# Agent attention with two MLPs on one core: a timetable's list drives the first sixteen steps and the weight conversions, without the clamp and without the pool engine

## The chip, the cores and the metric

The kernel runs on one core of a Trainium2 chip. The metric is the device time of one execution in microseconds, and every time here is of that kind. Five engines appear: TensorE (PE in the profile; PEld is its weight load), VectorE (DVE), ScalarE (ACT), GpSimd (POOL) and SyncE (SP), whose queue issues almost all DMAs.

## What is computed

The reference is an attention through 49 agents, and after it two feed-forward layers on all 12480 tokens of 128 channels:

```python
a2k = sm(agents, k)                 # 49 agents look at 12480 keys
agent_v = a2k @ v                   # 49 x 128
q2a = sm(q, agents)                 # each token looks at the 49 agents
x = q2a @ agent_v
x = maximum(x @ w_in, 0)**2 @ w_out             # first layer, 2048 hidden
h = x @ w_in2                                   # second layer, 2048 hidden
y = (maximum(h, 0) + alpha * minimum(h, 0)) @ w_out2
```

Here `sm` is a softmax over scaled products. The four weight matrices lie in DRAM as 64-bit floats, and the kernel makes 32-bit floats of them on the chip; everything else is float32.

## The kernel before

**The fold.** The product `agent_v @ w_in` is made once (49 x 2048, called W1), so that the first layer's hidden values of a token are its softmax row times W1. The leaky relu of the second layer is split into `(1-alpha) * relu(h)` and a linear part: w_out2 is scaled by 1-alpha (`oma`), and M = w_in2 · diag(alpha) · w_out2 (128 x 128) is made once and applied to x directly.

**Precision.** Operands of the large products are split into a high and a low part in the fp32r format (a cast, then a subtraction), and three products hi·lo, lo·hi, hi·hi are added up. So each operand costs a cast (ACT, or DVE for `g1h`) and a subtraction.

**The weights.** Each of the four matrices comes in four parts of 128x512 numbers, named `wi1.0` to `wo2.3` (in the trace all parts pass through the buffers raw, mag and wf). A part goes through these steps, each a letter ahead of its name in the order lists:
- d (`w_load`, L131 to L149): a 512 KB DMA into one of six `raw` slots, two int32 halves to a number;
- a (`w_abs`, L152, ACT): absolute value of the upper half, read as a float, into one of two `mag` slots;
- m (`w_max`, L156, POOL): a clamp from below at 2^-15, so that the exponent can be shifted in place;
- b (`w_bits`, L160, L161, L164, DVE): shift and mask, put the sign in, put the low half's bits in, to one of five `wf` slots; the `raw` and `mag` slots are free after it;
- s (`w_scale`, L392, POOL), for wo2 only: times 1-alpha, into another `wf` slot;
- h (`w_hi`, L399, ACT) and l (`w_lo`, L403, POOL): the high part and the low part, for wo1, wi2 and wo2 (W1 has its own, L649 on ACT and L652 on DVE);
- t, y (`m_transpose`, L415, PE; `m_alpha`, L421, DVE), for wi2: transposed, times alpha, into mT; z, w (`m_product`, PE; `m_add`, L439 and on, DVE): M's partial product and its sum.

**Attention.** Keys and values come in 13 chunks each (`ring<-in_k_dram`, `ring<-in_v_dram`, 512 KB apiece). A chunk of keys is transposed (T, C), multiplied with the agents (S), gets a running maximum and an exponential (X, P and the line L549, L553, L560), is turned (E, F: L570, L577) and multiplied with its chunk of values (M). At the end the 49 x 128 result is normalised (N, L620), transposed (vT) and copied as `avT` (vc, L635), from which W1 is made (W0, W1, with Y and Z for its two parts).

**The steps.** The tokens are cut into 25 blocks (320 tokens, then 512 each, 384 in the last), and each block takes 8 steps, 200 in all. A step s does H1 (first layer, products of W1 and the softmax rows `qsh`, `qsl` into `h_ps`), relu (L756, ACT), square (L876, ACT), G1 (cast L764 and subtraction L765, DVE), and, two steps later, O (the second product). Eleven steps behind H1 comes H2 of the second layer (relu L819 on ACT, L820 on DVE), and one step behind that its O. All matmuls go through `mm` (L78).

**What sets the order.** Scheduling is by hand: each engine executes its instructions in the order in which the program issues them. Before the loop a written list, ORDER, interleaves the attention, the first query blocks (names beginning with q) and the conversion of wi1 and wo1 and of a part of wi2. The rest of the conversions, of wi2 and wo2, stands in a table LATER, by the steps 0 to 13 behind which they are issued. Loads stand in the list too, so SP's queue follows it: its DMAs are issued in order, and one that waits for its slot holds those behind it.

**PSUM.** ORDER runs in a pool `early`; the loop's pool opens when ORDER is done, and with it the SBUF pools `wk` and `xp` of the loop.

Of the kernel before, what the change touches and what calls it, by code (L numbers as in the profile page):

```python
# [19 lines left out]
def agent_attention_moe_kernel(  # L20
# [96 lines left out]
    HI_KEEP = -(1 << 30)  # L117
    MIN_HI = 2.0 ** -15
# [4 lines left out]
    wf = Slots(stg, 5, [QW], F32, "wf")  # L123
# [46 lines left out]
    with tc.manual_schedule(), ExitStack() as first:  # L170
        early = first.enter_context(tc.tile_pool(name="early", bufs=1, space=PSUM))
# [218 lines left out]
        def w_scale(x):  # L390
            g = int(x[4:])
            nc.gpsimd.tensor_tensor(  # L392
# [14 lines left out]
        wT, mP = {}, {}  # L407
# [25 lines left out]
        def m_add(x):  # L433
            g = int(x[4:])
            p_ = mP.pop(g)
            if g == 0:
# [50 lines left out]
        kT_ps, kT_sb, s_ps, ex_sb, e_ps, e_sb, q_ps, out_ps = {}, {}, {}, {}, {}, {}, {}, {}  # L487
# [86 lines left out]
        def e_copy(c):  # L574
            p, t = shape(c)
            e_sb[c] = att.tile([128, KC // 2, 2, H], F32, tag="e1", name="e1", bufs=3)[:p, :t]
            nc.scalar.copy(e_sb[c].rearrange("p j r a -> p (j r a)"), e_ps.pop(c))  # L577

        def av_chunk(c):
            p, t = shape(c)  # L580
            g = GROUP[c]
            e, v_ = e_sb.pop(c), chunk("v", c)
# [101 lines left out]
        def q_end(b):  # L684
# [8 lines left out]
            "T": q_turn, "h": q_first_hi, "l": q_first_lo, "s": q_scores, "t": q_squares, "m": q_max, "u": q_sub,  # L693
# [240 lines left out]
```

## Time and profile before

| | us |
|---|---|
| runs | 1127.34, 1125.65, 1119.55 |
| median | 1125.65 |
| profiled execution | 1119.32 |
| its span in the trace | 1117.5 |
| around the span | 1.8 |
| mean granted PE clock | 0.982 |

The span is cut by the profile's page into 40 slices of 28 us. PE, at work nearly all the time, is not so only in the first six slices; the work that the change touches lies there. Where a busy time and a number of instructions stand together, the number is behind an x. "Granted clock" is the share of full speed (2.4 GHz) that PE was given; 0.5 is the lower of its two levels.

### The profile page before, as it was taken

The page shows a single profiled execution, that of the slowest core. Times are in us where ns is not written, and L with a number is a line of the kernel's source. Part 1 is how long each engine was busy: PE and PEld are TensorE (multiplying, and loading weights), DVE is VectorE, ACT ScalarE, POOL GpSimd, SP SyncE. Part 2 cuts the span into 40 slices and gives each one's busy share as a digit, 9 for nine tenths or more (in the row PEclk, how much of TensorE's full clock was granted, in tenths as well). Part 3 has the DMA queues.
Part 4 walks back from the last instruction along what each step waited for, and adds up shares of the span by engine and source line. Part 5 has one row for each costly group of instructions (what it writes and reads, how often), then busy time and mean ns, then how long its engine had stood idle before and what let it go on. Part 6 is the DMA issues. An engine that isn't in the chain of part 4 may idle for free.

```text
span 1117.5 us, 22093 instructions
## 1 busy us (share of the span) xinstructions
PE 1072.9 (96%) x9368; PEld 859.8 (77%) x9368; DVE 897.9 (80%) x1377; ACT 728.9 (65%) x835; POOL 46.8 (4%) x38
## 2 busy tenths in 40 slices
PE   8868699999999999999999999999999999999997
PEld 5546588888888888888888888888888888888886
DVE  6778787887887888887888788788788888788753
ACT  5656376666666666666667667666766676766642
POOL 1353300000000000000000000000000000000000
PEclk9978799999999999999999999999999999999999
DMA  9941011111111111111111111111111111001011
GB/s 348 322 126 23 1 30 17 29 34 22 27 35 29 20 29 30 20 29 29 20 30 29 20 29 32 17 31 37 20 26 33 29 18 29 20 11 29 20 24 18
DMA packets 119931, 48.19 MB, mean 43 GB/s; under 512 B 103640, under 2 KB 109337, under 8 KB 119833
## 3 DMA queue, kind: packets, MB, share of 16 engines
q1 hardware_dynamic: 119832, 46.79, 17.6%
q8 instruction: 73, 1.20, 0.5%
q14 instruction: 26, 0.20, 0.1%
HBM read 27.59 MB, written 6.39 MB: 30 GB/s over the span
## 4 chain that ended last, share of the span: by engine, by line
PE 88%; DVE 7%; ACT 2%; issue 1%; DMA 1%; SPq 0%; POOL 0%; DVEq 0%; ACTq 0%
PE o L78 49%; PE h_ps L78 36%; PE s_ps L78 2%; DVE g1l L765 1%; DVE mag L161 1%; PE M_ps L78 1%; DVE wf L164 1%; DVE g1h L764 1%; DVE mag L160 1%; DVE mx L549 0%; DVE g2l L820 0%; PE warm_ps L78 0%; SPq L244 0%; ACT kT L533 0%; ACT g L876 0%
## 5 line engine op out<-in xcount | busy, mean ns | idle before, releaser
L756 ACT ACTIVATE g<-h_ps 128x1024 f32<-128x1024 f32 (+2 forms) x200 | 201.0, 1005 | 177.3 <-PE h_ps L78 176.5
L819 ACT ACTIVATE g2h<-h_ps 128x1024 fp32r<-128x1024 f32 (+2 forms) x200 | 201.5, 1007 | 151.4 <-PE h_ps L78 132.7
L820 DVE SCALAR_TENSOR_TENSOR g2l<-h_ps,g2h 128x1024 fp32r<-128x1024 f32 (+2 forms) x200 | 238.2, 1191 | 21.0 <-ACT g2h L819 21.0
L765 DVE TENSOR_TENSOR g1l<-g,g1h 128x1024 fp32r<-128x1024 f32 (+2 forms) x200 | 242.6, 1213 | 6.9
L764 DVE CAST g1h<-g 128x1024 fp32r<-128x1024 f32 (+2 forms) x200 | 136.8, 684 | 111.5 <-ACT g L876 110.6
L876 ACT ACTIVATE g<-g 128x1024 f32<-128x1024 f32 (+2 forms) x200 | 207.8, 1039 | 6.4
L78 PE MATMUL o<-g1h,wo1l 64*128 64x512 f32 (+2 forms) x800 | 158.1, 392 | 0.0
L78 PE MATMUL o<-g2l,wo2h 64*128 64x512 f32 (+2 forms) x800 | 157.5, 389 | 0.5 <-DVE g2l L820 0.5
L78 PE MATMUL o<-g2h,wo2h 64*128 64x512 f32 (+2 forms) x800 | 157.5, 389 | 0.0
L78 PE MATMUL o<-g1h,wo1h 64*128 64x512 f32 (+2 forms) x800 | 157.4, 390 | 0.0
L78 PE MATMUL o<-g1l,wo1h 64*128 64x512 f32 (+2 forms) x800 | 157.1, 389 | 0.1
L78 PE MATMUL o<-g2h,wo2l 64*128 64x512 f32 (+2 forms) x800 | 156.4, 386 | 0.0
L78 PEld LDWEIGHTS o<-g1l,wo1h 64*128 64x128 f32 x800 | 76.4, 188 | 17.9 <-DVE g1l L765 0.3
L78 PEld LDWEIGHTS o<-g1h,wo1h 64*128 64x128 f32 x800 | 76.5, 188 | 17.3
L78 PEld LDWEIGHTS o<-g2h,wo2l 64*128 64x128 f32 x800 | 76.3, 186 | 17.3 <-ACT g2h L819 0.2
L78 PEld LDWEIGHTS o<-g2l,wo2h 64*128 64x128 f32 x800 | 75.9, 185 | 17.3 <-DVE g2l L820 0.8
L78 PEld LDWEIGHTS o<-g1h,wo1l 64*128 64x128 f32 x800 | 76.3, 187 | 16.8
L78 PEld LDWEIGHTS o<-g2h,wo2h 64*128 64x128 f32 x800 | 75.9, 185 | 16.4
L78 PE MATMUL h_ps<-qsh,W1l 64*128 64x512 f32 (+2 forms) x400 | 80.8, 401 | 7.3 <-DVE W1l L652 2.8
L78 PE MATMUL h_ps<-xh,wi2l 64*128 64x512 f32 (+2 forms) x400 | 79.3, 392 | 1.2 <-DVE g2l L820 1.2
L78 PE MATMUL h_ps<-sl,wi2h 64*128 64x512 f32 (+2 forms) x400 | 79.4, 390 | 0.4 <-DMA sl<-xl 0.4
L78 PE MATMUL h_ps<-sh,wi2l 64*128 64x512 f32 (+2 forms) x400 | 79.2, 389 | 0.4 <-DMA sh<-xh 0.4
(142 smaller groups left out, 1476.1 us busy)
## 6 DMA issues: line engine op xcount, KB each, us to landing
ring<-in_k_dram SPq DMA_DIRECT2D x12, 512.0 KB, 7.9
ring<-in_v_dram SPq DMA_DIRECT2D x12, 512.0 KB, 6.8
sh<-xh SPq DMA_DIRECT2D x46, 128.0 KB, 2.4
sl<-xl SPq DMA_DIRECT2D x46, 128.0 KB, 2.3
out_dram<-ot SPq DMA_DIRECT2D x92, 64.0 KB, 2.0
q_sb<-in_q_dram SPq DMA_DIRECT2D x176, 32.0 KB, 1.9
raw<-in_moe_w_in_dram SPq DMA_DIRECT2D x4, 512.0 KB, 10.0
raw<-in_moe_w_out_dram SPq DMA_DIRECT2D x4, 512.0 KB, 9.2
```

The source lines that it names most:

```text
L78: nc.tensor.matmul(o, lhsT, rhs, start=start, stop=stop)
L160: nc.vector.tensor_scalar(a, a, 3, 0x3FFFFFF8, op0=ALU.logical_shift_left, op1=ALU.bitwise_and)
L161: nc.vector.scalar_tensor_tensor(out=a, in0=hi, scalar=HI_KEEP, in1=a, op0=ALU.bitwise_and, op1=ALU.bitwise_or)
L164: nc.vector.scalar_tensor_tensor(out=dst.bitcast(I32), in0=lo, scalar=29, in1=a, op0=ALU.logical_shift_right, op1=ALU.bitwise_or)
L756: nc.scalar.activation(g, p_, AF.Relu)
L764: nc.vector.tensor_copy(gh, g)
L765: nc.vector.tensor_tensor(out=gl, in0=g, in1=f32(gh), op=ALU.subtract)
L819: nc.scalar.activation(gh, p_, AF.Relu)
L820: nc.vector.scalar_tensor_tensor(out=gl, in0=p_, scalar=0.0, in1=f32(gh), op0=ALU.max, op1=ALU.subtract)
L876: nc.scalar.activation(h1g[s], h1g[s], AF.Square)
```

## The change

One list now covers what ORDER and LATER held and the first sixteen steps (blocks 0 and 1) besides: H1 to H1_15, the first products O1 up to step 13, H2 up to step 4 and O2 up to step 3, and the third query block's softmax. The loop begins at step 16. For that the step functions are cut into pieces that a list can name (`H1_0`, `r1_0` relu, `s1_0` square, `c1_0` and `x1_0` G1's cast and subtraction, and so on). The order inside the list is new. The other edits:
- The absolute value is multiplied by 2^-112 (`REBIAS`), the clamp is gone, the shift has no mask, and the sign is taken with a mask of the top bit.
- `w_scale` (four instructions) and `w_lo` (twelve) are on DVE; nothing of the weights is left on POOL.
- `m_alpha`: each of its four DVE instructions of 128x512 becomes four on ACT of 128x128, with alpha as the scale of each partition.
- `wf` has six slots in place of five.
- M's partial products are added up in the order in which they come.
- The early PSUM pool closes before W1's product, which takes a bank of the loop's pool; the attention's SBUF pool closes at PART2.

```diff
-    wf = Slots(stg, 5, [QW], F32, "wf")
+    wf = Slots(stg, 6, [QW], F32, "wf")
...
     def w_abs(x):
-        nc.scalar.activation(mag.take(x).bitcast(F32), raw.get(x)[:, :, 1].bitcast(F32), AF.Abs)
-
-    def w_max(x):
-        m = mag.get(x).bitcast(F32)
-        nc.gpsimd.tensor_scalar(m, m, MIN_HI, None, op0=ALU.max)
+        nc.scalar.activation(mag.take(x).bitcast(F32), raw.get(x)[:, :, 1].bitcast(F32), AF.Abs, scale=REBIAS)
...
-        nc.vector.tensor_scalar(a, a, 3, 0x3FFFFFF8, op0=ALU.logical_shift_left, op1=ALU.bitwise_and)
+        nc.vector.tensor_scalar(a, a, 3, None, op0=ALU.logical_shift_left)
         nc.vector.scalar_tensor_tensor(
-            out=a, in0=hi, scalar=HI_KEEP, in1=a, op0=ALU.bitwise_and, op1=ALU.bitwise_or
+            out=a, in0=hi, scalar=SIGN, in1=a, op0=ALU.bitwise_and, op1=ALU.bitwise_or
         )
...
         def w_scale(x):
-            nc.gpsimd.tensor_tensor(
+            nc.vector.tensor_tensor(
...
+        LO_VECTOR = 'wo1.0 wo1.1 wo1.2 wo1.3 wi2.0 wi2.1 wi2.2 wi2.3 wo2.0 wo2.1 wo2.2 wo2.3'.split()
         def w_lo(x):
             hi, lo = halves(x)
-            nc.gpsimd.tensor_tensor(out=lo, in0=source(x), in1=f32(hi), op=ALU.subtract)
+            e = nc.vector if x in LO_VECTOR else nc.gpsimd
+            e.tensor_tensor(out=lo, in0=source(x), in1=f32(hi), op=ALU.subtract)
...
         def m_alpha(x):
-            a = alp.rearrange("p (i r) -> p r i", r=2)[:, :, 2 * g:2 * g + 2]
-            nc.vector.tensor_tensor(
-                out=mT[:, g], in0=wT.pop(g), in1=a.unsqueeze(3).to_broadcast([128, 2, 2, 128]), op=ALU.mult
-            )
+            p_ = wT.pop(g)
+            for i in range(2):
+                for r in range(2):
+                    k = 4 * g + 2 * i + r
+                    nc.scalar.activation(mT[:, g, r, i], p_[:, r, i], AF.Copy, scale=alp[:, k:k + 1])
...
         ORDER = """
...
+            R5 bwo1.3 hwo1.0 M11 dwo2.1 awo2.0 E12 hwi2.2 dwo2.2 R6 F12 N2 hwo1.3 M12 awi2.3 dwo2.3 R7 bwi2.3 vT
+            vc hwi2.3 lwo1.3 PART1 W0 awo2.3 bwo2.0 W1 Y0 Z0 awo2.1 swo2.0 PART2 H1_0 Y1 q2 lwo1.0 r1_0 Z1
...
-        LATER = {
...
+        S0 = 2 * NP
+        pend = [S0 - D - 1]
-        for s in range(S + D + 2):
+        for s in range(S0, S + D + 2):
...
-            for x in LATER.get(s, "").split():
-                step(x)
```

On DVE, around the begin of the steps (first the four H1 products of width 320: `g_888`, `g_864` and the like are the relu'd hidden values of one step each), the kernel before has this:

```order
L421 TENSOR_TENSOR mT<-wT_ps,alp 128x512
L652 TENSOR_TENSOR W1l<-w_ps,W1h 128x512 x2
L764 CAST g1h<-g_888 128x2x320
L765 TENSOR_TENSOR g1l<-g_888,g1h 128x2x320
L160 TENSOR_SCALAR mag<-mag 128x512
L161 SCALAR_TENSOR_TENSOR mag<-raw,mag 128x512
L164 SCALAR_TENSOR_TENSOR wf<-raw,mag 128x512
L764 CAST g1h<-g_915 128x2x320
L765 TENSOR_TENSOR g1l<-g_915,g1h 128x2x320
```

and the changed kernel this:

```order
L654 TENSOR_TENSOR W1l<-w_ps,W1h 128x512
L389 TENSOR_TENSOR wf<-wf,oma 128x512
L403 TENSOR_TENSOR wo1l<-wf,wo1h 128x512
L654 TENSOR_TENSOR W1l<-w_ps,W1h 128x512
L156 TENSOR_SCALAR mag<-mag 128x512
L157 SCALAR_TENSOR_TENSOR mag<-raw,mag 128x512
L160 SCALAR_TENSOR_TENSOR wf<-raw,mag 128x512
L770 CAST g1h<-g_864 128x2x320
L775 TENSOR_TENSOR g1l<-g_864,g1h 128x2x320
L770 CAST g1h<-g_897 128x2x320
L775 TENSOR_TENSOR g1l<-g_897,g1h 128x2x320
L403 TENSOR_TENSOR wi2l<-wf,wi2h 128x2x256
```

The alpha product left DVE, a scale (L389) and low parts (L403) joined it, and a conversion now stands ahead of the first step's cast where it stood behind its subtraction.

On ACT at the same place, from W1's high parts to the first steps' relu and square, before:

```order
L649 CAST W1h<-w_ps 128x512
L399 CAST wi2h<-wf 128x2x256
L649 CAST W1h<-w_ps 128x512
L152 ACTIVATE mag<-raw 128x512
L756 ACTIVATE g_888<-h_ps 128x2x320
L876 ACTIVATE g_888<-g_888 128x2x320
L756 ACTIVATE g_915<-h_ps 128x2x320
L876 ACTIVATE g_915<-g_915 128x2x320
```

and in the changed kernel:

```order
L651 CAST W1h<-w_ps 128x512
L152 ACTIVATE mag<-raw 128x512
L651 CAST W1h<-w_ps 128x512
L759 ACTIVATE g_864<-h_ps 128x2x320
L396 CAST wo2h<-wf 128x512
L763 ACTIVATE g_864<-g_864 128x2x320
L759 ACTIVATE g_897<-h_ps 128x2x320
L763 ACTIVATE g_897<-g_897 128x2x320
L424 ACTIVATE mT<-wT_ps,alp 128x128 x4
L759 ACTIVATE g_932<-h_ps 128x2x320
```

A high part (L396) now stands between the first step's relu and its square, and the four alpha products (L424) ahead of the third step's relu.

On SP, its queue from the second part of wo1 on, before:

```order
L141 DMA raw<-in_moe_w_out_dram 128x4x256
L481 DMA ring<-in_k_dram 128x1024 x2
L481 DMA ring<-in_v_dram 128x1024 x2
L141 DMA raw<-in_moe_w_out_dram 128x4x256 x2
L139 DMA raw<-in_moe_w_in_dram 64x512 x16
L149 DMA raw<-in_moe_w_out_dram 128x2x256 x8
L244 DMA q_sb<-in_q_dram 32x8x32 x24
```

and in the changed kernel from the first part of wi2 on (`64x512` is a quarter of a part of wi2, L149 half a part of wo2):

```order
L139 DMA raw<-in_moe_w_in_dram 64x512 x4
L483 DMA ring<-in_k_dram 128x1024
L141 DMA raw<-in_moe_w_out_dram 128x4x256
L483 DMA ring<-in_v_dram 128x1024 x2
L139 DMA raw<-in_moe_w_in_dram 64x512 x8
L141 DMA raw<-in_moe_w_out_dram 128x4x256
L483 DMA ring<-in_v_dram 128x1024
L149 DMA raw<-in_moe_w_out_dram 128x2x256 x2
L483 DMA ring<-in_v_dram 128x1024
L139 DMA raw<-in_moe_w_in_dram 64x512 x4
L483 DMA ring<-in_v_dram 128x1024
L149 DMA raw<-in_moe_w_out_dram 128x2x256 x6
```

The last chunks of K and V stood ahead of all loads of wi2 and wo2; now all of wi2 and a part of wo2 stand ahead of the last V chunk.

## Rows read from the trace of the kernel before

**Rows 1.** Page: busy us, share of the span and instructions by engine.
```profile
PE 1072.9 (96%) x9368; PEld 859.8 (77%) x9368; DVE 897.9 (80%) x1377; ACT 728.9 (65%) x835; POOL 46.8 (4%) x38
```

**Rows 2.** Windows: us, busy PE, PEld, DVE, ACT, POOL, PEclk, DMA share, GB/s.
```profile
7.23:148.03 140.80, 106.73 (x921) 78.50 (x921) 112.21 (x220) 82.76 (x129) 46.08 (x32) 0.87 0.47 153
146.22:1117.50 971.28, 961.93 (x8446) 779.99 (x8442) 785.82 (x1146) 645.54 (x703) 0.00 (x0) 1.00 0.14 26
...
77.00:102.00 25.00, 18.00 (x184) 15.11 (x184) 21.36 (x33) 18.65 (x26) 8.39 (x6) 0.85 0.18 28
102.00:137.90 35.90, 24.85 (x166) 20.11 (x166) 27.99 (x44) 14.49 (x19) 13.25 (x10) 0.74 0.04 10
```

**Rows 3.** Timeline of PE: start, duration, what; the bracket: idle before it, releaser.
```profile
134.32 1.16 PE L78 MATMUL M_ps<-wf,mT 128*128 128x128 f32 x8 [3.79 <-DVE g2l L820]
135.86 2.08 PE L78 MATMUL M_ps<-wf,mT 128*128 128x128 f32 x8 [0.38 <-DVE Mf L439]
137.86 0.79 PE L78 MATMUL h_ps<-qsh,W1l 64*128 64x512 f32 x2
146.22 0.40 PE L78 MATMUL h_ps<-qsh,W1l 64*128 64x512 f32 x2
```

**Rows 4.** Waits, 7.23 to 148.7: engine, line, releaser: us, times, longest.
```profile
PE M_ps L78 <- DVE g2l L820: 10.0, 2, 6.2
...
DVE g1h L764 <- ACT g L876: 6.9, 5, 2.4
DVE mx L549 <- PE s_ps L78: 6.3, 3, 2.9
...
DVE agTh L508 <- ACT agT L501: 4.3, 1, 4.3
```

**Rows 5.** Groups by form on DVE, 7.23 to 148.03: busy us, mean ns | idle before.
```profile
L161 DVE SCALAR_TENSOR_TENSOR mag<-raw,mag 128x512 int32<-128x512 int32 x16 | 12.1, 755 | 0.5
L765 DVE TENSOR_TENSOR g1l<-g,g1h 128x1024 fp32r<-128x1024 f32 x8 | 11.7, 1461 | 0.3
L765 DVE TENSOR_TENSOR g1l<-g,g1h 128x640 fp32r<-128x640 f32 x8 | 7.6, 947 | 0.3
...
L553 DVE SCALAR_TENSOR_TENSOR nm<-mx,nm 128x1 f32<-128x1 f32 x7 | 3.0, 422 | 0.2
L421 DVE TENSOR_TENSOR mT<-wT_ps,alp 128x512 f32<-128x512 f32 x4 | 2.7, 686 | 1.6 <-PE wT_ps L415 1.6
L370 DVE TENSOR_TENSOR qsl<-e,qsh 128x512 fp32r<-128x512 f32 x2 | 1.4, 680 | 0.0
```

**Rows 6.** Timeline of DVE: start, duration, what.
```profile
50.25 0.16 DVE L553 SCALAR_TENSOR_TENSOR nm<-mx,nm 128x1 f32<-128x1 f32 x1
...
50.95 0.69 DVE L161 SCALAR_TENSOR_TENSOR mag<-raw,mag 128x512 int32<-128x512 int32 x1
...
82.82 0.82 DVE L765 TENSOR_TENSOR g1l<-g,g1h 128x640 fp32r<-128x640 f32 x1
84.09 1.80 DVE L765 TENSOR_TENSOR g1l<-g,g1h 128x640 fp32r<-128x640 f32 x1
...
98.41 1.23 DVE L765 TENSOR_TENSOR g1l<-g,g1h 128x1024 fp32r<-128x1024 f32 x1
```

**Rows 7.** Timeline of POOL: start, duration, what, idle before it and releaser.
```profile
83.74 1.46 POOL L403 TENSOR_TENSOR wi2l<-wf,wi2h 128x512 fp32r<-128x512 f32 x1 [5.48 <-ACT wi2h L399]
```

**Rows 8.** Windows: the attention, ended by 69.12, and two within; columns as in rows 2.
```profile
7.23:69.12 61.89, 48.83 (x449) 32.46 (x447) 49.58 (x124) 38.68 (x69) 20.05 (x14) 0.96 0.89 310
10.00:20.00 10.00, 8.84 (x93) 5.58 (x93) 6.57 (x21) 6.40 (x13) 1.49 (x1) 1.00 1.04 397
40.00:50.00 10.00, 6.53 (x50) 3.72 (x47) 6.95 (x11) 5.50 (x9) 2.44 (x3) 1.00 1.04 328
```

**Rows 9.** Page, DMA issues: how often, KB each, us to landing.
```profile
ring<-in_v_dram SPq DMA_DIRECT2D x12, 512.0 KB, 6.8
```

**Rows 10.** Groups by form on ACT, 7.23 to 148.03: busy us, mean ns | idle.
```profile
L577 ACT COPY e<-e_ps 96x128 f32<-96x128 f32 x1 | 0.3, 261 | 1.1 <-PE e_ps L570 1.1
```

More of the change, by code (lines that the diff above doesn't have):

```diff
@@ L170, in agent_attention_moe_kernel @@
     with tc.manual_schedule(), ExitStack() as first:
-        early = first.enter_context(tc.tile_pool(name="early", bufs=1, space=PSUM))
+        early_pool = first.enter_context(ExitStack())
+        early = early_pool.enter_context(tc.tile_pool(name="early", bufs=1, space=PSUM))
         att = first.enter_context(tc.tile_pool(name="att", bufs=1))
@@ L435, in m_add @@
             p_ = mP.pop(g)
-            if g == 0:
+            if not m_done:
                 nc.vector.tensor_copy(Mf, p_[:, :C])
@@ L581, in av_chunk @@
             g = GROUP[c]
-            e, v_ = e_sb.pop(c), chunk("v", c)
+            e, v_ = e1_sb.pop(c), chunk("v", c)
             for j in range(t):
@@ L641, in w1_product @@
             if g == 0:
-                out_ps["w1"] = early.tile([128, 2, NT], F32, tag="kT", name="w1_ps")
+                out_ps["w1"] = ps("h2", "w1_ps")
             p_ = out_ps["w1"][:, g].rearrange("p (i m) -> p i m", m=128)
@@ L708, in step @@
                 weight(x)
+            elif "_" in x:
+                LOOP[x[:2]](int(x[3:]))
+            elif x[:2] in X_STEPS:
+                X_STEPS[x[:2]](int(x[2:]))
             elif x[0] == "q":
-                if x[1].isdigit():
-                    q_first(int(x[1]))
+                if not x[1].isdigit():
+                    Q_STEPS[x[1]](int(x[2:]))
+                elif int(x[1:]) < 2:
+                    q_first(int(x[1:]))
                 else:
-                    Q_STEPS[x[1]](int(x[2:]))
+                    q_load(int(x[1:]))
             elif x[0] in "KV":
@@ L791, in X1_add, with X1_part, X1_swap, X1_hi @@
             nc.vector.tensor_tensor(out=x1[b], in0=x1[b], in1=o1p.pop(b)[:, 1], op=ALU.add)
-        def X1(b):
+        def X1_part(b, tag, swapped):
+            return [pools["xp"].tile([128, NT], F32R, tag=t, name=t)[:, :width(b)] for t in (tag, swapped)]
+        def X1_swap(a, o):
+            for r in range(2):
+                nc.sync.dma_start(out=f32(o[rows(r)]), in_=f32(a[rows(1 - r)]))
+        def X1_hi(b):
             x = x1[b]
-            n = width(b)
-            xh, sh, xl, sl = (xp.tile([128, NT], F32R, tag=t, name=t)[:, :n] for t in ("xh", "sh", "xl", "sl"))
+            xh, sh = X1_part(b, "xh", "sh")
             nc.scalar.copy(xh, x)
+            X1_swap(xh, sh)
+            x1[b] = x, xh, sh
+        def X1_lo(b):
+            x, xh, sh = x1[b]
+            xl, sl = X1_part(b, "xl", "sl")
             nc.vector.tensor_tensor(out=xl, in0=x, in1=f32(xh), op=ALU.subtract)
-            for a, o in ((xh, sh), (xl, sl)):
-                for r in range(2):
-                    nc.sync.dma_start(out=f32(o[rows(r)]), in_=f32(a[rows(1 - r)]))
+            X1_swap(xl, sl)
             x1[b] = (xh, sh), (xl, sl)
@@ L842, in agent_attention_moe_kernel @@
+        """
+        for x in ORDER.split():
+            step(x)
         before = {
@@ L880, in agent_attention_moe_kernel @@
                 X1_copy(bx)
-            if i == 1 and s >= NP:
+            if i == 1:
                 q_scores(b + 1)
@@ L897, in agent_attention_moe_kernel @@
                 OUT(bo)
-            for f, ahead in after.get(i, ()) if s >= NP else after_0.get(i, ()):
+            for f, ahead in after.get(i, ()):
                 f(b + ahead)
@@ L901, in agent_attention_moe_kernel @@
                 q_load(b + 3)
-            for x in LATER.get(s, "").split():
-                step(x)
 _INS = ["q", "k", "v", "agents", "moe_w_in", "moe_w_out", "moe2_w_in", "moe2_w_out", "moe2_alpha"]
```

143 lines of the change are left out of this document (81 added, 62 removed).

## Prediction

> **What bounds the kernel now.** I read first the busy times of the engines: PE is at work for 1072.9 us, far ahead of DVE's 897.9 [rows 1]. So I looked next for where PE is not busy. The windows say it: from 146.22 us on, where H1 of step 16 starts, PE works 961.93 of 971.28 us at full clock [rows 2]. The code behind that point is the same in both kernels, since the new loop begins with that step. What the change can win or lose is the place of that one matmul in time: the time after is 1119.3 (the profiled execution's own) less 146.2, plus the time at which step 16's H1 starts, plus what that stretch loses behind it.
>
> Then I asked who sets the 146.2. From 7.23 to 148.03 DVE is busy 112.21 of 140.80 us, PE 106.73 at a mean clock of 0.87, ACT 82.76, POOL 46.08 [rows 2]. No engine is full; DVE comes nearest. The list of waits agrees: PE's longest ones for M's products are for DVE, 10.0 us in two waits, and DVE itself waits for ACT's squares (6.9) and for PE's scores (6.3) [rows 4]. I read the stretch as DVE's work plus DVE's waits, 112.2 and 28.6, in an order that lets neither cover the other.
>
> Third, DVE's own groups. Some durations are too long for their size: the subtraction L765 of 128x640 takes 0.947 on average [rows 5], but 0.82 alone at 82.82 and 1.80 at 84.09 [rows 6], when POOL was at a subtraction from 83.74 to 85.20 [rows 7]. L553, one column wide, takes 0.422 on average and 0.16 alone [rows 5, 6]. DVE loses time beside POOL.
>
> **The change part by part, on DVE.** Its work before is 112.2.
> - Added: 12 low parts and 4 scales, 128x512 each, from POOL. The nearest row is L370, the same operation, size and types: 680 ns [rows 5]; 16 x 0.68 = 10.9. From below, 0.82 for 640 columns scaled to 512 gives 0.66, so 10.5; from above, the disturbed 0.947 gives 15.2. I take 10.9.
> - Removed: four alpha products, 4 x 0.686 = 2.7 [rows 5].
> - Stretches that go with POOL's work, mean less alone [rows 5, 6]: L765 of 1024, 8 x (1.461 - 1.23) = 1.85; L765 of 640, 8 x (0.947 - 0.82) = 1.0; L553, 7 x (0.422 - 0.16) = 1.8; L161, 16 x (0.755 - 0.69) = 1.0. Together 5.7.
> - The shift has one operation instead of two. No row shows that form. Of a part's three DVE instructions the dearest row is L161's 0.755; a third off that for 16 parts would be 4.0 won, and equally much lost if the single form were dearer. I take 0, as the size and the types stay.
>
> Sum: 112.2 + 10.9 - 2.7 - 5.7 = 114.7.
>
> On the stretches the Trainium skill ("SBUF — State Buffer", section "SBUF: two separate sides") has a rule: DVE and GpSimd share a port pair as an exclusive lock, held for a whole instruction, and a DVE operation with two SBUF inputs meets it. By the rule all such stretches end with an idle POOL, and the sum would be the 114.7; if they had another cause it would be 120.4, a rival below. The 1.80 against 0.82 speaks for the rule.
>
> **DVE's waits** were 28.6. The order on record shows the means to cut them: a conversion (three instructions that need only a landed weight) stands ahead of the first step's cast, where DVE before went from conversion to cast and back only between steps. Waits of the kind that such work fills are the 6.9 and the 6.3 [rows 4]. The 4.3 for the agents' transpose [rows 4] stands at the very start, before a part of the weights has been converted, and stays. So the bounds are 4.3 below and 28.6 - 13.2 = 15.4 above; I take 6, near the lower end, as stretches of the groups that I did not list still sit inside the 114.7 and come off too. DVE starts at 7.2, so it is through at 7.2 + 114.7 + 6 = 127.9, and I let step 16's H1 start there: 18.3 earlier.
>
> **The other engines.** ACT gets 16 products of 128x128 for alpha. The nearest row is a copy of 96x128, 261 ns [rows 10]: 16 x 0.26 = 4.2, at worst 16 x 0.69 = 11. ACT is idle for 58 of 140.8 us [rows 2], which hides either; behind them in its queue stands the third step's relu, so if they come late PE's H1 bank is late by the four of them, 1.0. The scale in the absolute value is an argument of the same instruction: 0, and the clamp's instructions were POOL's, whose idleness costs nothing but ends one link of each conversion. The sixth wf slot and the order of M's sum remove waits only. The pool PART1 opens earlier makes W1's product wait for the last users of the early banks; it waited for them before as well: 0.
>
> SP's queue is where the change takes a risk: all of wi2 and a part of wo2 stand ahead of the last V chunk. By my count 20 MB must then have landed before the attention can end. In full use the DMA engines moved 397 GB/s at 10 to 20 us and 328 at 40 to 50 [rows 8]: 50 or 61 us from 7.2 on, so V's last chunk lands between 58 and 68. Before, the attention ended at 69.1, with DVE busy 49.58 of 61.89 [rows 8]; with its waits cut it would end near 62. I take the faster end, since the contiguous K and V chunks carry most bytes, and charge nothing.
>
> **PE's clock.** When PE stands still the granted clock falls and what follows is slow: M's product takes 2.08 where the one before took 1.16, and H1's first pair at 137.86 takes 0.79 against 0.40 at 146.22 [rows 3]. A list that keeps DVE full will still leave PE short of work for a while, and some of that return to full clock may fall behind the common point: four such matmul pairs, 4 x 0.39, are 1.5 lost.
>
> In all 18.3 - 1.5 = 16.8, so 1119.3 - 16.8 = 1102.5; I say 1102. The profiled execution lies at the low end of the runs, 6 below their median of 1125.65; a median that stood so to it would be 1108, within the range. About 1% (11.3 us) is what a measurement of this kernel can tell from no change, so faster means below 1114.4. With the bounds of the main case (waits 4.3 to 15.4, prices -0.4 to +4.3, the shift ±4) it goes from 1096 to 1112 and, with wholly unlisted stretches, to 1090.
>
> **Rivals.**
> *The loads come late.* For it: the mean of the whole attention was 310 GB/s, not 397 [rows 8], and 20 MB at that rate take 64.5 us, so V's end lands at 71.7 where I need some 62. Against it: the engines were in full use in both stretches, so the mean holds waits for slots. Price 71.7 - 62 = 9.7: 1112.
> *The change does not do what it says*: the stretches were not POOL's. Then 5.7 come back: 1108. Against it are the two L765 side by side [rows 6, 7].
> *PE at its lower clock becomes the bound.* PE's work from 77 to 137.9 is 18.00 x 0.85 + 24.85 x 0.74 = 33.7 at full clock [rows 2], and 8.4 follow to 146.22 [rows 3]: 42.1, or 84.2 at the lower level, 1.2 GHz. If the attention ends at 62 and PE never has work enough to be raised, step 16 starts at 62 + 84.2 = 146.2, as before: 1119. For it: in 102 to 137.9, where PE was busy 24.85 of 35.9, the clock was 0.74 [rows 2]. Against it: at 40 to 50 PE was busy 6.53 of 10 at 1.00 [rows 8], and a denser list keeps it busier than now.
> The Trainium skill ("TensorE: Matmul & The Clock Gate", section "Part 1: The HAM clock gate") puts it that "the default state is throttled, and activity releases the throttle". The 0.74 agrees; the 1.00 at a busy share below it does not by itself.
> *Slower: the SP queue blocks.* A weight's load waits for a raw slot that only a DVE conversion frees; with seven such loads ahead of K or V chunks, each wait holds a chunk, and the conversion that would free the slot is queued on DVE behind attention work that needs the chunk. One held chunk costs at most its landing, 6.8 [rows 9]: 7 x 6.8 = 47.6, less what DVE can convert meanwhile, six slots of 3 x 0.755 = 13.6, makes 34 and 1136. It decides against the change from 16.8 us of net waits on; by 28 it is slower by over 1%. Against it: six raw slots, as before, and a list that places each conversion.
>
> **How the numbers follow.** Main 0.68, late loads 0.14, stretches not POOL's 0.06, lower clock 0.08, blocked queue 0.04. Faster by over 1% are the main case, the stretches and part of the late loads: 0.80. Within 1%: the rest of the late loads and the lower clock, 0.15. Slower: 0.05. The range, 1090 to 1118, holds the first three and leaves out the clock's and the queue's, and the outer ends of the main one.
>
> **What would show it.** Step 16's H1 near 128 in place of 146.2. DVE busy for about 115 from 7 to there, with L765 of 640 at 0.82 and 1024 at 1.23, and the low parts at 0.68. DVE's waits below 15. The attention's last copy (avT) near 62; if it is at 69 or later and the last V chunk is what it waited for, the loads were the rival. A clock below 0.7 from the first step to step 16 with PE busy throughout shows the clock's. I am wrong if DVE has over 25 us of waits there, or if PE is no longer full behind step 16.

## The result, and the profile after

The changed kernel takes 1108.26 us (median of four runs, 1106.78 to 1109.29) against 1126.05 for the kernel before (the three runs above and a fourth of 1126.44): a ratio of 0.9852, 95% interval 0.9813 to 0.9892. It is faster, by 1.5%; 1102 was forecast, in a range of 1090 to 1118. The profiled execution took 1108.75 with a span of 1106.9, which is 10.6 less than the span before. That the medians lie 17.8 apart and the two traces 10.6 comes from the runs of the kernel before, and is looked at below.

The page's busy times of the changed kernel answer to [rows 1]:

```profile
PE 1072.7 (97%) x9368; PEld 857.5 (77%) x9368; DVE 893.0 (81%) x1389; ACT 732.2 (66%) x851; POOL 0.7 (0%) x6
```

PE's work is the same, and POOL is empty as the change says. The windows answer to [rows 2] (same columns). Step 16's H1 starts at 133.35 here and avT's copy at 70.60:

```profile
7.20:133.35 126.15, 102.67 (x905) 73.69 (x903) 106.14 (x230) 85.20 (x144) 0.00 (x0) 0.91 0.57 173
133.35:1106.90 973.55, 963.98 (x8442) 780.90 (x8442) 784.88 (x1146) 644.94 (x701) 0.00 (x0) 1.00 0.13 26
7.20:70.60 63.40, 51.74 (x449) 34.37 (x447) 49.66 (x131) 40.25 (x73) 0.00 (x0) 0.89 1.01 325
70.60:133.35 62.75, 50.93 (x456) 39.32 (x456) 56.47 (x101) 44.95 (x71) 0.00 (x0) 0.92 0.12 21
```

For the kernel before, the stretch from avT's copy to step 16 in the same view:

```profile
69.12:146.22 77.10, 56.09 (x456) 44.50 (x458) 60.82 (x96) 42.64 (x59) 26.03 (x18) 0.79 0.13 29
```

So the 12.9 by which step 16 comes earlier are not spread over the stretch. The attention ends 1.5 later than before. Everything is won behind it: 62.75 for 77.10, that is 14.4. There DVE's work fell from 60.82 to 56.47 and its idle time from 16.3 to 6.3, and PE's mean clock rose from 0.79 to 0.92. The last two move together in most runs below, and no run sets the clock by itself: which of them drives the other is not shown. Behind step 16 2.3 are lost (973.55 for 971.28).

DVE's groups by form answer to [rows 5] (columns: busy us, mean ns | idle before):

```profile
L157 DVE SCALAR_TENSOR_TENSOR mag<-raw,mag 128x512 int32<-128x512 int32 x16 | 11.1, 693 | 0.5
L775 DVE TENSOR_TENSOR g1l<-g,g1h 128x1024 fp32r<-128x1024 f32 x8 | 9.8, 1224 | 0.2
...
L775 DVE TENSOR_TENSOR g1l<-g,g1h 128x640 fp32r<-128x640 f32 x8 | 6.6, 825 | 0.3
...
L403 DVE TENSOR_TENSOR wi2l<-wf,wi2h 128x512 fp32r<-128x512 f32 x4 | 2.7, 686 | 0.0
...
L555 DVE SCALAR_TENSOR_TENSOR nm<-mx,nm 128x1 f32<-128x1 f32 x7 | 1.1, 159 | 0.2
```

These are the lone durations of [rows 6], each within 10 ns: 693 for 0.69, 1224 for 1.23, 825 for 0.82, 159 for 0.16. The low part, new on this engine, takes the 0.68 of L370.

Why the attention ended late is read from three timelines of the changed kernel. PE's (start, duration, what, in brackets the idle time before it and its releaser), at an earlier chunk of values, the last three, and step 16:

```profile
41.48 1.09 PE L78 MATMUL av_ps<-ring,e 128*64 128x128 f32 x16
...
58.98 1.97 PE L78 MATMUL av_ps<-ring,e 128*64 128x128 f32 x16 [4.45 <-DMA ring<-in_v_dram]
...
62.76 1.98 PE L78 MATMUL av_ps<-ring,e 128*64 128x128 f32 x16 [0.76 <-ACT e L579]
...
66.53 1.97 PE L78 MATMUL av_ps<-ring,e 128*64 128x128 f32 x16 [0.75 <-ACT e L579]
...
133.35 0.50 PE L78 MATMUL h_ps<-qsh,W1l 64*128 64x512 f32 x2 [2.12 <-ACT qsh L361]
```

SP's (the duration is the time that the issue took):

```profile
43.30 9.89 SPq L139 DMA_DIRECT2D raw<-in_moe_w_in_dram  x8
53.30 0.52 SPq L141 DMA_DIRECT2D raw<-in_moe_w_out_dram  x1
53.92 0.45 SPq L483 DMA_DIRECT2D ring<-in_v_dram  x1
```

and ACT's:

```profile
55.58 0.66 ACT L152 ACTIVATE mag<-raw 128x512 f32<-128x512 f32 x1 [3.06 <-DMA raw<-in_moe_w_in_dram]
...
58.02 0.57 ACT L579 COPY e<-e_ps 128x512 f32<-128x512 f32 x1
```

Two parts of wi2 hold SP's queue for 9.9 us; the V chunk for which PE waits until 58.98 is issued behind them, at 53.92. At the same time ACT stands before an absolute value whose weight has not landed, and the copy of e, which belongs to the attention, is queued behind it. After the stop PE runs at its lower clock: 16 of these matmuls take 1.97, which were 1.09 at 41.48. The window from 60 to 70 us (columns as in [rows 2]) has the clock at 0.50:

```profile
60.00:70.00 10.00, 7.79 (x52) 5.68 (x48) 5.70 (x20) 3.98 (x8) 0.00 (x0) 0.50 1.08 301
```

### The profile page after: what moved, and what is told of

It reads as the page before. It is cut to its first block, busy times and chain, and to the rows that moved or that the text cites. A ratio compares the mean times of both kernels' runs of the same rounds, so it can differ in the third digit from the quotient of the medians.

```text
span 1106.9 us, 22085 instructions
## 1 busy us (share of the span) xinstructions
PE 1072.7 (97%) x9368; PEld 857.5 (77%) x9368; DVE 893.0 (81%) x1389; ACT 732.2 (66%) x851; POOL 0.7 (0%) x6
## 4 chain that ended last, share of the span: by engine, by line
PE 89%; DMA 5%; DVE 4%; ACT 1%; issue 1%; SPq 0%; DVEq 0%; ACTq 0%
PE o L78 49%; PE h_ps L78 36%; PE s_ps L78 2%; DMA raw<-in_moe_w_in_dram 2%; DMA ring<-in_k_dram 1%; DMA ring<-in_v_dram 1%; DVE g1l L775 1%; DMA sl<-xl 1%; DVE g1h L770 1%; DMA raw<-in_moe_w_out_dram 1%; DVE g2l L849 0%; PE kT_ps L529 0%; PE w_ps L78 0%; PE M_ps L78 0%; PE av_ps L78 0%
## 5 line engine op out<-in xcount | busy, mean ns | idle before, releaser
L775 DVE TENSOR_TENSOR g1l<-g,g1h 128x1024 fp32r<-128x1024 f32 (+2 forms) x200 | 239.7, 1199 | 6.8
L78 PEld LDWEIGHTS o<-g2h,wo2h 64*128 64x128 f32 x800 | 75.8, 184 | 16.3
```

Of the source, the lines that this page charges most:

```text
L78: nc.tensor.matmul(o, lhsT, rhs, start=start, stop=stop)
L775: nc.vector.tensor_tensor(out=gl, in0=g, in1=f32(gh), op=ALU.subtract)
```

## The experiments

All stand on the changed kernel, except the old order's and the two repeats of the kernel before. Times and ratios are medians and comparisons of runs. Each ratio is to runs of the kernel before taken beside that kernel, whose median lay between 1122.64 and 1126.05, so that ratios compare better between the kernels than times do; the other columns are read from each profiled execution: avT's copy, step 16's H1, the stretch between the two with DVE's busy and idle time in it, and the span behind step 16.

| kernel | us | ratio to before (95%) | avT | step 16 | between: length, DVE busy, idle | behind |
|---|---|---|---|---|---|---|
| before | 1126.05 | | 69.12 | 146.22 | 77.10, 60.82, 16.28 | 971.28 |
| changed | 1108.26 | 0.9852 (0.9813 to 0.9892) | 70.60 | 133.35 | 62.75, 56.47, 6.28 | 973.55 |
| old order, new operations | 1118.17 | 0.9945 (0.9927 to 0.9963) | 66.57 | 143.02 | 76.45, 58.37, 18.08 | 971.28 |
| new order, old operations | 1121.67 | 0.9981 (0.9963 to 0.9999) | 71.48 | 144.94 | 73.46, 61.97, 11.49 | 973.66 |
| clamp on POOL | 1110.44 | 0.9875 (0.9832 to 0.9919) | 71.44 | 134.93 | 63.49, 57.26, 6.23 | 973.67 |
| low parts, scales on POOL | 1111.75 | 0.9894 (0.9857 to 0.9932) | 69.26 | 136.19 | 66.93, 55.22, 11.71 | 973.31 |
| alpha product on DVE | 1112.48 | 0.9892 (0.9857 to 0.9927) | 71.98 | 139.19 | 67.21, 58.87, 8.34 | 973.71 |
| V's loads first | 1110.81 | 0.9885 (0.9849 to 0.9922) | 71.91 | 135.11 | 63.20, 56.24, 6.96 | 973.59 |
| conversions late | 1104.78 | 0.9821 (0.9789 to 0.9854) | 66.16 | 129.32 | 63.16, 58.30, 4.86 | 973.68 |
| q pieces early | 1108.64 | 0.9854 (0.9820 to 0.9887) | 70.38 | 135.77 | 65.39, 56.49, 8.90 | 971.63 |
| wi2 in rows | 1102.40 | 0.9820 (0.9797 to 0.9844) | 62.07 | 125.04 | 62.97, 56.27, 6.70 | 974.36 |
| two DMAs a part | 1125.66 | 1.0024 (1.0011 to 1.0038) | 82.64 | 150.20 | 67.56, 58.24, 9.32 | 973.40 |

### The order and the operations, each alone

The old order with the new operations:

```diff
-        nc.scalar.activation(mag.take(x).bitcast(F32), raw.get(x)[:, :, 1].bitcast(F32), AF.Abs)
...
-        nc.gpsimd.tensor_scalar(m, m, MIN_HI, None, op0=ALU.max)
...
+        nc.scalar.activation(mag.take(x).bitcast(F32), raw.get(x)[:, :, 1].bitcast(F32), AF.Abs, scale=REBIAS)
...
-            nc.gpsimd.tensor_tensor(out=lo, in0=source(x), in1=f32(hi), op=ALU.subtract)
+            nc.vector.tensor_tensor(out=lo, in0=source(x), in1=f32(hi), op=ALU.subtract)
```

(`w_scale`, `w_bits` and `m_alpha` as in the change; ORDER and LATER as before, without the clamp's entries.)

> The kernel before with its own order and loop, and all the edits of operations: scaled absolute value, no clamp, single shift, low parts and scales on DVE, alpha product on ACT, POOL idle. Theory A (the edits bring DVE's busy time down by some 4 to 6 us but its waits of 28 stay): step 16's H1 at 140 to 146, time 0 to 6 below the kernel before. Theory B (the edits carry the change, the order little): time as the changed kernel's, ratio about 0.985.

The new order with the old operations (the token "m" behind each "a" of the list, `LO_VECTOR` empty, the scale on POOL, the old `m_alpha`):

> The changed kernel's order with the old operations: clamp on POOL directly behind each absolute value, low parts and scales on POOL, alpha product on DVE. Theory A (the order carries the change): step 16's H1 at 134 to 139, time 0 to 6 above the changed kernel's, ratio 0.985 to 0.990. Theory B (the order pays only with an idle POOL): H1 of step 16 at 143 or later, ratio 0.995 or more.

The first gained 0.55% and the second 0.19%, both together 1.48%, twice their sum; by the traces' spans they are 3.2, -1.1 and 10.6 us. In the first, theory A held: step 16's H1 at 143.02, DVE 5.1 us less busy from 7.2 on (105.28 for 110.40), but idle behind avT for 18.1, no less than before. In the second, theory B held, at 144.94: DVE's busy time went up to 114.24, its idle time behind avT fell only to 11.5, and the attention ended at 71.48.

```profile
7.20:144.94 137.74, 101.81 (x903) 72.83 (x901) 114.24 (x216) 81.82 (x128) 47.08 (x32) 0.91 0.51 159
```

POOL is busy for 47.08 us in it, and DVE does 8.1 more than in the changed kernel, though 16 instructions fewer are its own from the weights and only four more from alpha. What follows: the order is worth much only where operations take the times and places that it was laid out for; the operations are worth much only in an order that lets DVE use what they free.

### POOL's two kinds of work, and alpha

```diff
-        LO_VECTOR = 'wo1.0 wo1.1 wo1.2 wo1.3 wi2.0 wi2.1 wi2.2 wi2.3 wo2.0 wo2.1 wo2.2 wo2.3'.split()
+        LO_VECTOR = []
...
         def w_scale(x):
             g = int(x[4:])
-            nc.vector.tensor_tensor(
+            nc.gpsimd.tensor_tensor(
```

> The changed kernel, with the 12 low parts and the 4 scales back on POOL, the order unchanged. Theory A (POOL's work costs DVE about what it saves it): DVE's own work falls by 10.9, the stretches give most of that back, H1 of step 16 within 2 us of 133.4, time within 2 us of the changed kernel's. Theory B (DVE bounds the stretch behind avT and the stretches are small): H1 of step 16 near 127, time 5 to 7 lower. Theory C (a low part on POOL is 1.3 to 1.5 long and is waited for, since the order was made for 0.68): time 3 to 8 higher.

It came out between A and C: 3.5 slower by median, which is C's price (the intervals of the ratios overlap), step 16 2.8 later, and DVE's busy time much as A has it. From 7.20 to step 16 DVE is busy for this:

```profile
7.20:136.19 128.99, 103.66 (x900) 73.70 (x899) 104.69 (x213) 85.04 (x144) 22.09 (x16) 0.89 0.54 169
```

Sixteen instructions of 10.9 us in all left DVE, and its busy time fell by 1.45 (106.14 to 104.69). The rest came back as stretches, for 22.09 us of POOL's work: the instructions that stayed on DVE, summed by form, are longer by 8.3. (DVE's instructions overlap a little, so durations add up to somewhat more than busy time.) The group that showed it before shows it again; and a low part takes POOL twice what it takes DVE:

```profile
L775 DVE TENSOR_TENSOR g1l<-g,g1h 128x640 fp32r<-128x640 f32 x8 | 8.0, 1005 | 0.3
```

```profile
L403 POOL TENSOR_TENSOR wo2l<-wf,wo2h 128x512 fp32r<-128x512 f32 x4 | 6.8, 1699 | 8.4 <-ACT wo2h L396 8.4
```

So the rival that the stretches are not POOL's has fallen, and moving POOL's work to DVE costs DVE 1.5, not 10.9. The rest of the loss is idle time, 11.7 for 6.3 behind avT.

The clamp alone (`w_max` on POOL behind each absolute value, the two-operation shift):

> The changed kernel's order with the old conversion: clamp on POOL behind each absolute value, two-operation shift, all else new. Theory A (POOL's clamp stretches DVE's operations and lengthens each conversion by 1.5, for which DVE then waits in its fixed order): DVE busy up by 3 to 5, its waits behind avT up too, step 16's H1 at 138 to 141, time 1112 to 1116. Theory B (the clamp's latency is covered by the order): H1 of step 16 within 2 of 133.4, time within 2 of the changed kernel's.

Nearer to B: step 16's H1 1.6 later, time 2.2 higher with intervals that overlap, DVE busy for 107.86 (1.7 more). POOL is busy for 25.67 us with the 16 clamps, more than with the low parts and scales, and DVE pays 1.7 for them. Twelve of the clamps stand ahead of avT, where the attention waits for loads anyway (DVE has 13.7 idle in the changed kernel there), and four behind it. Whether the clamps are cheap by their place or by their kind (they read one tile, the low parts and scales two) was not tested.

```diff
         def m_alpha(x):
             g = int(x[4:])
-            p_ = wT.pop(g)
-            for i in range(2):
-                for r in range(2):
-                    k = 4 * g + 2 * i + r
-                    nc.scalar.activation(mT[:, g, r, i], p_[:, r, i], AF.Copy, scale=alp[:, k:k + 1])
+            a = alp.rearrange("p (i r) -> p r i", r=2)[:, :, 2 * g:2 * g + 2]
+            nc.vector.tensor_tensor(
+                out=mT[:, g], in0=wT.pop(g), in1=a.unsqueeze(3).to_broadcast([128, 2, 2, 128]), op=ALU.mult
+            )
```

> The changed kernel with the alpha product back on DVE (four instructions of 128x512 in place of sixteen on ACT), the order unchanged. Theory A (behind avT the stretch is DVE's work plus its waits): DVE's work rises by 4 x 0.69 = 2.7, step 16's H1 1 to 3 us later than 133.4, time 1109 to 1111. Theory B (ACT's queue is as tight there): no difference or up to 2 faster.

Theory A by its direction, but larger: step 16's H1 at 139.19, 5.8 later. Of it 1.4 lie ahead of avT, where nothing was edited; behind avT DVE is busy for 2.4 more and idle for 2.1 more. Why four instructions of 0.68 bring idle time of nearly their own length is not settled; the clock there is 0.84 against 0.92. The profiled execution is also the slowest of its four (1114.68, the others 1111.13 to 1113.01); by the medians the loss is 4.2.

### Where the attention's end comes from

```diff
-            dwi2.1 awo1.2
+            awo1.2
...
-            bwi2.0 awi2.2 dwo2.0 M9 A6 P6 E10 X7 awo1.3 V11 F10 N0 P7 M10 dwi2.3 bwi2.2 N1 A7 E11 hwi2.0 V12 F11
+            bwi2.0 awi2.2 M9 A6 P6 E10 X7 awo1.3 V11 F10 N0 P7 M10 bwi2.2 N1 A7 E11 hwi2.0 V12 dwi2.1 dwi2.3 dwo2.0 F11
```

> The changed kernel, with the loads of wi2.1, wi2.3 and wo2.0 moved behind the last V chunk in SP's order; nothing else moves. Theory A (the last V chunks come late because wi2's loads stand ahead of them): the 4.45 us for which PE waited for a V chunk at 58.98 go, avT's copy comes at about 66 instead of 70.6, step 16's H1 at about 129 instead of 133.4, and the time is 4 to 5 us under the changed kernel's, ratio to before about 0.981. Theory B (the end of the attention is set by the e, copy, av chain at PE's lower clock and by ACT's queue, not by landings): avT moves by less than 1.5 us and the time stays at the changed kernel's, ratio about 0.985.

Neither held. PE's wait for V went, and another took its place two chunks later; the view is PE's timeline, then the waits from 7 to 136 us (us, times, longest):

```profile
56.53 1.09 PE L78 MATMUL av_ps<-ring,e 128*64 128x128 f32 x16 [2.83 <-ACT e L579]
...
67.83 1.98 PE L78 MATMUL av_ps<-ring,e 128*64 128x128 f32 x16 [7.26 <-ACT e L579]
```

```profile
ACT mag L152 <- DMA raw<-in_moe_w_out_dram: 8.3, 3, 6.8
```

ACT had to take wo2.0's absolute value ahead of the last e copy, and wo2.0 now landed later. The two queues hold the same chain: here the load that was moved back is the one that ACT's order needs ahead of the attention's end. So the next run moves the load and the conversion that waits for it:

```diff
-            dwi2.1 awo1.2
+            awo1.2
...
-            bwi2.0 awi2.2 dwo2.0 M9 A6 P6 E10 X7 awo1.3 V11 F10 N0 P7 M10 dwi2.3 bwi2.2 N1 A7 E11 hwi2.0 V12 F11
-            R5 bwo1.3 hwo1.0 M11 dwo2.1 awo2.0 E12 hwi2.2 dwo2.2 R6 F12 N2 hwo1.3 M12 awi2.3 dwo2.3 R7 bwi2.3 vT
-            vc hwi2.3 lwo1.3 PART1 W0 awo2.3 bwo2.0 W1 Y0 Z0 awo2.1
+            bwi2.0 awi2.2 M9 A6 P6 E10 X7 V11 V12 dwi2.3 dwo2.0 awo1.3 F10 N0 P7 M10 bwi2.2 N1 A7 E11 hwi2.0 F11
+            R5 bwo1.3 hwo1.0 M11 dwo2.1 E12 hwi2.2 dwo2.2 R6 F12 N2 hwo1.3 M12 dwo2.3 R7 dwi2.1 vT
+            vc lwo1.3 awi2.3 PART1 W0 awo2.0 bwi2.3 W1 Y0 hwi2.3 awo2.3 bwo2.0 Z0 awo2.1
```

> The changed kernel with the last V chunks ahead of wi2.1, wi2.3 and all of wo2 in SP's order, and besides with the absolute values of wi2.3 and wo2.0 and their conversions moved behind avT's copy, so that neither ACT nor DVE stands behind a load that has not landed. Theory A (attention's end was held by conversions queued ahead of it on ACT and DVE, whose loads were late): avT's copy at 63 to 66 in place of 70.6, step 16's H1 at 127 to 131 (the moved conversion costs DVE some 2 behind avT), time 1102 to 1106. Theory B (the chain through PE, ACT and the running sum sets it): avT at 69 or later, time 1108 or more.

Theory A, at step 16 and in time; avT at 66.16 is just past its 66:

```profile
7.20:66.16 58.96, 51.49 (x447) 33.77 (x444) 47.55 (x127) 40.24 (x73) 0.00 (x0) 0.92 1.04 336
66.16:129.32 63.16, 50.93 (x458) 39.19 (x458) 58.30 (x103) 44.51 (x71) 0.00 (x0) 0.92 0.17 32
```

The stretch behind avT is as long as in the changed kernel with 1.8 more of DVE's work in it, so its idle time is 4.9. It beats both kernels: 1104.78 (1104.31 to 1104.84), no run of which overlaps with those of the changed kernel, though the intervals of the two ratios do.

What wi2's loads cost by their shape, with amount and order unchanged (the second layer's first weights are then other numbers of the matrix than the reference asks for):

```diff
-        if name == "wi1":
+        if name in ("wi1", "wi2"):
```

One DMA of 128 partitions and 4 KB rows takes the place of four of 64 partitions and 2 KB pieces.

> The changed kernel, with each part of wi2 loaded by one DMA in rows of 4 KB (a part of wi2's own rows in their place, so the second layer's weights are not the ones asked for) in place of four DMAs in pieces of 2 KB; amount and order unchanged. Theory A (the four small DMAs hold SP's queue, 9.9 us for eight of them, and with it the last V chunks): V's chunk for the wait at 58.98 lands 3 to 6 earlier, avT's copy at 65 to 68, step 16's H1 at 128 to 131, time 1103 to 1106. Theory B (the bytes ahead of V's chunks count, not their shape): avT at 70 to 71, time within 2 of the changed kernel's.

Theory A, and beyond it. avT's copy comes at 62.07, step 16 at 125.04. The first row is the changed kernel's in the second half of the eight small DMAs' issue, when little else is landing, the second this one's at 30 to 50 us, where all four parts of wi2 are issued among other loads:

```profile
48.00:53.00 5.00, 3.64 (x35) 2.29 (x35) 4.19 (x10) 4.05 (x8) 0.00 (x0) 1.00 0.80 173
```

```profile
30.00:50.00 20.00, 19.54 (x180) 12.60 (x180) 17.41 (x43) 15.82 (x28) 0.00 (x0) 1.00 1.04 388
```

With wi2 in rows all loads together move 388 GB/s; the small DMAs alone move 173 (253 over the whole of their 9.9 us, in which other loads still land). PE is busy for 47.71 of the 54.87 us up to avT (51.74 of 63.40 in the changed kernel), and its clock there is 1.00. By place this is the largest single price found: 8.5 us of attention. By ratio the run is like the one with late conversions (0.9820 and 0.9821). The run doesn't separate the shorter hold of SP's queue from the faster landing.

The price could have been read before the change. In the kernel before, the same small DMAs ran behind the last V chunk, all 16 in a row, and the two views (SP's timeline, then a window) give their rate:

```profile
43.13 15.41 SPq L139 DMA_DIRECT2D raw<-in_moe_w_in_dram  x16
```

```profile
50.00:58.00 8.00, 7.62 (x83) 5.89 (x82) 4.74 (x11) 7.30 (x14) 3.18 (x3) 1.00 0.68 176
```

The last run keeps wi2's own layout: late conversions, and for each half h of a part one DMA over all 128 partitions, from a source of 2 x 64 x 512.

```diff
-            src = w.rearrange("(h c) (r g x) -> r h g c x", h=2, r=2, g=4)
-            for r in range(2):
-                dst = t_[rows(r)].rearrange("p (h i m) w -> p h (i m w)", h=2, i=2)
-                for h in range(2):
-                    nc.sync.dma_start(out=dst[:, h], in_=src[r][h][g])
+            src = w.rearrange("(h c) (r g x) -> h g r c x", h=2, r=2, g=4)
+            dst = t_.rearrange("p (h i m) w -> h p (i m w)", h=2, i=2)
+            for h in range(2):
+                nc.sync.dma_start(out=dst[h], in_=src[h, g])
```

> The list of the run with late conversions, and each part of wi2 loaded by two DMAs over all 128 partitions in place of four over 64; the pieces stay at 2 KB, and the same numbers land in the same places. Theory A (the half of the partitions that each small DMA reaches is what slows wi2's loads to about 173 GB/s): the attention's loads go at 380 GB/s or more, avT's copy at 60 to 64, step 16's H1 at 123 to 127, time 1099 to 1103. Theory B (the 2 KB pieces do it, or the loads are no longer in the way once V's chunks stand ahead): within 1.5 of the run with late conversions alone, 1104.8.

Both theories fell: it is the slowest of the edited kernels, 0.24% behind the kernel before (0.11 to 0.38%), with avT at 82.64. Its windows while such a DMA runs:

```profile
52.00:58.00 6.00, 4.96 (x29) 2.86 (x30) 2.59 (x6) 4.82 (x9) 0.00 (x0) 0.60 0.13 49
```

A DMA share of 0.13 is as much as two of sixteen engines would give (0.125), at 49 GB/s. The source's outermost dimension is 2. The Trainium skill ("DMA: Bandwidth & Descriptors", section "Rules for kernel authors") has it that a copy whose outermost dimension is c, below 16, goes to at most c engines; the row agrees. For the 64-partition form the skill ("SBUF — State Buffer", section "Door 1: The DMA port swizzle") says that 64 partitions reach half of the ports, and gives 196 GB/s; the 173 lie near it, but 2 KB pieces and 64 partitions were changed together here, so which of them slows wi2's loads is open.

### Step 16's own stop, and the kernel before once more

```diff
-            lwo2.0 s1_15 H2_2 ql2 O2_0 c1_15 O2_1 r2_2 x1_15 qs2 x2_2 qt2 O2_2 qT3 H2_3 qm2 qh3 r2_3 qu2 x2_3
-            qe2 qz2 O2_3 H2_4 qn2 r2_4 x2_4 qH2 qL2
+            lwo2.0 s1_15 H2_2 ql2 qs2 O2_0 c1_15 qt2 O2_1 r2_2 x1_15 qm2 qu2 x2_2 qe2 O2_2 qz2 H2_3 r2_3 qn2 x2_3
+            qH2 qL2 O2_3 H2_4 qT3 qh3 r2_4 x2_4
```

> The changed kernel with the last softmax pieces of query block 2 moved some places forward in the list's end, and the turn of block 3 moved to its end. Theory A (PE's stop of 2.12 before step 16's H1 is for that softmax's row, and the lower clock behind it costs 2 more): H1 of step 16 at 131 in place of 133.4, the rest behind it 971.5 in place of 973.6, time 3 to 4 lower. Theory B (DVE is full there, another wait takes its place): within 1 of the changed kernel's.

Theory B. The span behind step 16 is 971.63, near the 971.28 of before, but step 16 comes 2.4 later: PE now stops for DVE's x2, and the lower clock that follows the stop (0.50 from 129.0 to 135) lies ahead of step 16 instead of behind it. The stop in PE's timeline:

```profile
128.31 0.41 PE L78 MATMUL o<-g2l,wo2h 64*128 64x320 f32 x2 [2.66 <-DVE g2l L849]
```

The kernel before, twice more, for the spread of its runs:

> The kernel before once more, for its trace. Theory A (its runs differ in the stretch ahead of step 16, by PE's granted clock or by the waits for M's products): the rest behind step 16's H1 is 971.3 again, and H1 of step 16 lies between 146 and 154, as the time lies between 1119 and 1127. Theory B (they differ behind it): H1 of step 16 at 146.2 within 1, the rest up to 979.

> The same as the run before it, a second look. Theory A: time less 973 gives step 16's H1 within 1 us. Theory B: step 16's H1 at 146.2 within 1.

The first took 1121.30, the second 1126.77. Step 16's H1 stands at 146.41 and 151.86, and behind it lie 973.1 in both, 1.8 more than in the first trace. The first bears out theory B; the second bears out neither (time less 973 is 153.8). Of the 7.5 that the second's span has over the first trace's, 4.1 lie between avT and step 16, 1.5 ahead of avT and 1.9 behind step 16:

```profile
70.67:151.86 81.19, 58.76 (x457) 47.62 (x459) 62.05 (x96) 42.81 (x59) 25.56 (x18) 0.77 0.13 28
```

DVE's idle time there is 19.1, against 16.3 [rows 2] and 15.3 in the other two. The stretch that the change shortens is thus the one that varies in the kernel before (77.1, 77.6, 81.2), and the trace on which the forecast was made had caught it at its shortest.

The 1.8 behind step 16 do not lie where the changed kernel's 2.3 lie. In the issues of the outputs the first repeat is 0.19 behind the first trace at the first one, 0.42 shortly before the end and 2.0 at the last. PE's clock is at its lower level there for a while, with PE at work throughout (first and second repeat, then the first trace):

```profile
1091.00:1093.00 2.00, 2.00 (x14) 2.00 (x12) 0.00 (x0) 0.61 (x1) 0.00 (x0) 0.50 0.03 8
1096.00:1098.00 2.00, 2.00 (x12) 2.00 (x12) 0.00 (x0) 0.00 (x0) 0.00 (x0) 0.50 0.03 8
1090.00:1092.00 2.00, 2.00 (x24) 2.00 (x22) 0.00 (x0) 0.79 (x1) 0.00 (x0) 1.00 0.04 8
```

The changed kernel has its lower clock right behind step 16:

```profile
135.35:137.35 2.00, 2.00 (x14) 1.67 (x12) 0.35 (x1) 1.59 (x2) 0.00 (x0) 0.50 0.00 0
```

So the column "behind" of the table adds up two different losses, and like numbers in it need not have a like cause. Why the clock falls near the end of some executions only is open.

## Why the prediction was right, and by which steps it was not

**The common point** held. Behind step 16 the two kernels run alike: at the first output's issue the changed kernel leads the first trace of before by 10.73, at the last by 10.60, and in between by 10.56 to 10.74 at all but six of the 100 issues (10.04 to 11.81). The loss at the restart was 2.3 for the 1.5 forecast, 2.1 of it ahead of the first output's issue: PE stops for 2.12 before step 16, and from about 135 us on it runs at the lower clock for a while.

**Prices on DVE** held one by one: low parts 0.686 for 0.68, the four stretched groups back to their lone times. The sum did not. From 7.2 to step 16 DVE was busy for 106.14, not 114.7. Of the 112.2 some 1.8 lie behind step 16 (110.40 up to it); the remaining 6.8 are stretches of groups that were not listed, such as G1's cast of 128x1024, which fell by 8 x (0.830 - 0.690) = 1.1. In all 110.40 + 10.9 - 2.7 - 106.14 = 12.5 of stretches went, where 5.7 were counted: the mechanism was right and its size too small, by taking four groups for all. In the old order it is as much, 110.40 + 10.9 - 2.7 - 105.28 = 13.3, so the stretches went with the operations and not with the order.

**DVE's waits** are the step that failed: 6 were taken in a range of 4.3 to 15.4, and 20.0 came (126.15 less 106.14). Behind avT the list did what was forecast, 16.3 to 6.3. Ahead of it nothing was won: 12.3 became 13.7. The sentence that failed is on SP's queue: "I take the faster end, since the contiguous K and V chunks carry most bytes, and charge nothing". K and V do carry most bytes, but directly ahead of the last V chunks stand wi2's small DMAs, which move 173 GB/s and not 397, and ACT's queue held the same chain a second time. avT came at 70.60 in place of 62; with wi2 in rows it came at 62.07. That this run's 1102.4 is also the number of the forecast is partly luck: its step 16 comes at 125.04, 2.9 earlier than forecast, and it needs 974.36 behind it, where the forecast has 971.3 and 1.5.

**The rivals.** The loads came late, as the first of them said: 8.6 for its 9.7. It did not end at its 1112 because the sum on DVE was 8.6 too high at the same time; the two errors offset in part, and step 16 came 5.4 later than forecast (133.35 for 127.9). That the stretches were not POOL's fell with the run on low parts. PE's lower clock appears (0.50 from 60 to 70 us), but as a result of late loads; behind avT the clock is 0.92. The blocked queue, priced at 6.8 for each of seven loads, cost one wait of 4.45 and one of 3.06.

**The signs** that the text named came out mixed. The lone durations held, the clock's rival did not show, and PE is full behind step 16. DVE's busy time of about 115 (106.1), its waits below 15 (20.0) and avT near 62 (70.6) failed; avT past 69 was the sign of late loads. The 25 us of waits from which the text would have called itself wrong were not reached. The main case's upper end, 1112, holds only the waits at their bound: with the prices (4.3) and the shift (4.0) at theirs too it would be 1120, outside the range of 1118.

**The footing.** The sum stood on one execution at the low end of the runs, and the text put a median that stood so to it at 1108. The gain by the traces is 10.6 for 16.8 forecast; by the medians it is 17.8. That the 17.8 lies near the 16.8 is luck: it comes from which execution of the kernel before was profiled. So is the 1108, since the changed kernel's trace (1108.75) does not lie low among its runs as was assumed. What held of the account is the mechanism, that less work beside POOL and fewer waits on DVE bring step 16 forward; its two sizes were off by 8.6 one way and 14.0 the other.

## What to carry to other kernels

Before an in-order list is made denser, ask of each load in it not only how many bytes stand ahead of it but in what shape: loads in pieces of 2 KB to 64 partitions, and loads with a short outermost dimension, ran at 173 and 49 GB/s where 388 was to be had, and held everything issued behind them. The rate of such a load is best read where it runs alone, in the trace of the kernel before. An instruction that waits for a late load holds its whole engine, so a load and the conversion that reads it are moved together. And operations and order are priced together: here they gave 0.55% and 0.19% alone, and 1.48% as a pair.

## What the runs showed of the hardware that was not expected

- Handing 10.9 us of DVE's work to POOL took only 1.45 us off DVE's busy time: POOL worked 22.09 us for it, and the durations of DVE's other instructions grew by 8.3. The 16 clamps, 25.67 us of POOL's work, added only 1.7 to DVE's busy time. One-input instructions grew as well: the cast of 128x1024 was 0.82 to 0.83 beside POOL and 0.69 without it.
- A DMA to 128 partitions whose source is 2 x 64 x 512 moved 49 GB/s at a DMA share of 0.13.
- Three executions of the kernel before differed by 4.1 us in the one stretch between avT and step 16 (77.1 to 81.2), and by under 2 in each of the other parts.
- Two of the three had PE at its lower clock near the end (0.50 at 1091 to 1093 and 1096 to 1098 us) with PE busy for all of the stretch; the third was at 1.00.
